# Per-head sums of six row groups moved from TensorE matmuls to SBUF-to-SBUF copies and VectorE adds

## The chip, the core and the metric

One core of one Trainium2 chip runs the whole program. The metric is the device time of one execution in microseconds (us).

## The reference, cut to what matters

Two layers, each an attention block A and a dense block B, over 2048 rows of 1024 values. Every row attends, in 32 heads of 32 channels, to eight rows: itself and the rows 2, 4, ..., 14 above.

```python
x = x + _A_ref(_layernorm(x), A_wqkv, A_wo)      # and again for layer 2
x = x + _B_ref(_layernorm(x), B_w1, B_b1, B_w2, B_b2)
# A: q, k, v = split(x @ wqkv); W, dil = 8, 2
logits = einsum("bhsd,bhswd->bhsw", q, kg) * Dh ** -0.5    # kg: k of the 8 rows
o = einsum("bhsw,bhswd->bhsd", softmax(logits), vg)        # then o @ wo
# B: gelu(x @ w1 + b1) @ w2 + b2, with F = 3584
```

## The kernel before

The rows are cut into groups of 512; `n` = 0 to 7 counts them, four in each layer. Tiles in PSUM take the results of TensorE; the other tiles here lie in SBUF. A group goes through four stages on TensorE: `gen_qkv`, `gen_wo`, `gen_ffn1`, `gen_ffn2`. Stages of different groups alternate, so that TensorE has matmuls while VectorE does the attention of another group. From group 1 on the order is wo(n), qkv(n+2), FFN1(n), FFN2(n). A stage yields after every unit of matmuls (8 matmuls in qkv, wo and FFN1; 7 in FFN2), and `sides` lists what is emitted after which unit. `hold()` makes all later VectorE instructions follow the last one emitted; otherwise the scheduler may reorder, and then each engine runs its list in order.

The channels lie so that the four partitions 4h to 4h+3 hold head h, in eight chunks `c`. A logit is therefore a sum over chunks, made by VectorE in `new_prod`, and a sum over four neighbouring partitions: the head sum. Before, TensorE makes it with a 0/1 matrix `smat` of 128x32, one quarter of the array for each 128 rows of the group:

```python
def head_sum(n, last=True):
    ...                                       # L: a PSUM tile [128, 8, 128], f32
    prod = st[n]["prods"].pop(0)
    for wh in range(2):
        for tb in range(NTT):                 # NTT = 4
            mm(L[tb * H:(tb + 1) * H, wh * 4:(wh + 1) * 4, :], lhsT=smat[:],
               rhs=prod[:, wh * 4:(wh + 1) * 4, tb * P:(tb + 1) * P], start=start,
               stop=last, skip_group_check=True, tile_position=(0, tb * H))

def attend(n):                                # softmax over the 8 rows
    head_sum(n); L = s.pop("L")
    ...                                       # mask for the first rows
    mx = max over w of L;  e = L - mx         # VectorE
    act.activation(e[:], e[:], ACT.Exp, scale=SCALE)      # ScalarE
    z = sum over w of e;  a = e / z           # VectorE (cut)
# spread(n): a goes through DRAM to all channels, abc     (GpSimd's DMA queue)
# av(n, c):  oT[c] = sum over w of abc * v, 4 VectorE ops (the weighted sums)
```

The schedule that the change touches (`ln_a(n)` normalizes the rows of group n and transposes them by DMA into `xnT`, which qkv(n) needs):

```python
stage(gen_ffn1(0), sides=at(4, attend, 1) + at(4, spread, 1) + at(4, hold) + each(new_prod, 2, 2, 1, 0, 4) + each(av, 1, 6, 2))
stage(gen_ffn2(0), sides=at(0, ln_stats_ahead, 3) + at(15, hold) + each(new_prod, 2, 15, 1, 4, 8) + at(23, hold) + at(23, ln_a, 3, None, True))
for n in range(1, N - 2):
    stage(gen_wo(n), sides=at(0, spread, n + 1) if n > 1 else at(7, attend, 2))
    stage(gen_qkv(n + 2), sides=(at(0, spread, 2) if n == 1 else []) + each(av, n + 1, 0, 2, 0, 3))
    stage(gen_ffn1(n), sides=at(20 if n == 1 else 9, attend, n + 2) + each(av, n + 1, 8, 2, 3, 8))
    if n + 3 < N:
        stage(gen_ffn2(n), sides=at(2, ln_a, n + 3))
    ...
```

## Time and profile before

| | before |
|---|---|
| device time, median of 6 runs | 1237.99 us (1237.62 to 1238.59) |
| span of the profiled run | 1236.0 us |
| TensorE / VectorE / ScalarE / GpSimd busy | 99% / 68% / 25% / 7% |
| granted TensorE clock | 1.00 |

The engine totals on the profile's page: busy us, share of the span, instructions.

```profile
PE 1227.6 (99%) x5775; PEld 632.1 (51%) x5825; DVE 840.5 (68%) x868; ACT 303.8 (25%) x475; POOL 92.3 (7%) x214
```

TensorE (PE) is never short of work, so only work or waits taken from it can change the time. The waits of PE in the whole run (who waited for whom: us in total, times, longest):

```profile
PE L L118 <- DVE big L93: 1.1, 1, 1.1
PE acc L118 <- DVE big L93: 1.1, 1, 1.1
PE acc L118 <- ACT xnT L93: 0.6, 1, 0.6
```

The last two are at the very start. The first is the head sum of group 1, as PE's timeline shows (start us, length us, engine, line, operation, tiles, count, idle before):

```profile
159.41 0.62 PE L118 MATMUL L<-big,smat 128*32 128x512 bf16 x8 [1.06 <-DVE big L93]
159.96 5.35 PE L118 MATMUL acc<-xnT,wt 128*128 128x512 bf16 x24
```

What a head sum costs is best read where nothing else disturbs. In FFN1, ScalarE applies one GELU per 8 matmuls and always waits for PE. Its timeline around the head sum of group 4:

```profile
472.32 0.69 ACT L93 ACTIVATE hT<-acc,b1T 128x512 bf16<-128x512 f32 x1 [1.04 <-PE acc L118]
474.05 0.69 ACT L93 ACTIVATE hT<-acc,b1T 128x512 bf16<-128x512 f32 x1 [1.04 <-PE acc L118]
476.43 0.69 ACT L93 ACTIVATE hT<-acc,b1T 128x512 bf16<-128x512 f32 x1 [1.69 <-PE acc L118]
```

The starts are 1.727 us apart, but 2.38 us across the head sum: it costs TensorE 0.65 us, more than the 0.55 us between its first start (159.41) and the next matmul's (159.96) in the timeline above.

### The profile page before, as it was taken

What the parts mean: (1) busy time and instruction counts of PE and PEld (TensorE: products, weight loads), DVE (VectorE), ACT (ScalarE), POOL (GpSimd) and SP (SyncE); (2) the same over time, 40 slices, a digit from 0 to 9 for tenths busy, and PEclk for the clock granted to TensorE, in tenths of its full rate; (3) what the DMA queues carried; (4) which work ended last, traced back from release to release, by engine and by line L of the source; (5) the groups of instructions that cost most, each with busy time, mean ns of one, the idle gap of its engine ahead of it and who ended that gap; (6) DMA issues with size and microseconds to landing.
All of it is one profiled execution on the core that took longest, in us unless ns stands there. A gap on an engine that the chain in (4) does not pass through costs nothing.

```text
span 1236.0 us, 13961 instructions
## 1 busy us (share of the span) xinstructions
PE 1227.6 (99%) x5775; PEld 632.1 (51%) x5825; DVE 840.5 (68%) x868; ACT 303.8 (25%) x475; POOL 92.3 (7%) x214
## 2 busy tenths in 40 slices
PE   9999999999999999999999999999999999999998
PEld 6666544456444564445644455444654444444444
DVE  7999899987985899337994379853597787012001
ACT  3333152023420145101351023510234001300310
POOL 4010011002000100001000010000001002000000
PEclk9999999999999999999999999999999999999999
DMA  9954564576645555656556565666554567546441
GB/s 305 283 179 144 187 208 155 166 177 220 183 157 200 168 175 157 195 168 189 166 155 203 171 178 162 162 200 200 171 170 136 185 199 200 162 157 196 150 136 54
DMA packets 217440, 220.33 MB, mean 178 GB/s; under 512 B 68179, under 2 KB 187105, under 8 KB 214305
## 3 DMA queue, kind: packets, MB, share of 16 engines
q1 hardware_dynamic: 214704, 208.69, 54.4%
q0 software_dynamic: 2672, 10.76, 2.9%
q8 instruction: 45, 0.74, 0.2%
q14 instruction: 19, 0.15, 0.0%
HBM read 197.40 MB, written 6.29 MB: 165 GB/s over the span
## 4 chain that ended last, share of the span: by engine, by line
PE 96%; DVE 2%; DMA 1%; issue 0%; POOL 0%; ACT 0%; SPq 0%
PE acc L118 96%; DVE big L93 1%; DVE stats L93 1%; DMA x<-in_A_x_dram 1%; PE L L118 0%; POOL rstd L93 0%; DVE x L93 0%; DVE xn L93 0%; SPq L93 0%; DVE mv L93 0%; ACT xnT L93 0%; PE L L211 0%; ACT kT L93 0%; ACT vT L93 0%; POOL zhalo L93 0%
## 5 line engine op out<-in xcount | busy, mean ns | idle before, releaser
L118 PE MATMUL acc<-xnT,wt 128*128 128x512 bf16 (+1 forms) x3376 | 721.5, 376 | 0.6 <-ACT xnT L93 0.6
L118 PEld LDWEIGHTS <-wt 128*128 128x128 bf16 x3376 | 398.7, 119 | 321.0 <-issue 3.9
L118 PE MATMUL acc<-wt,hT 128*128 128x512 bf16 (+1 forms) x1780 | 386.0, 376 | 2.1
L118 PEld LDWEIGHTS <-hT 128*128 128x128 bf16 x1820 | 178.1, 98 | 209.0
L93 DVE TENSOR_TENSOR big<-big 128x1024 bf16<-128x1024 bf16 (+2 forms) x184 | 244.1, 1358 | 1.8
L93 ACT ACTIVATE hT<-acc,b1T 128x512 bf16<-128x512 f32 x224 | 151.5, 687 | 318.4 <-PE acc L118 317.8
L93 DVE TENSOR_TENSOR big<-abc,vT 128x4096 bf16<-128x4096 bf16 x64 | 143.9, 2282 | 48.2 <-DMA abc<-a_d 47.9
L93 DVE TENSOR_TENSOR tmp<-acc,b2bc 128x512 f32<-128x512 f32 x56 | 38.6, 690 | 179.1 <-PE acc L118 175.7
L93 DVE TENSOR_TENSOR big<-qT,kT 128x4096 bf16<-128x4096 bf16 x64 | 143.8, 2286 | 23.9 <-ACT kT L93 23.2
L93 ACT CAST qT<-acc 128x512 bf16<-128x512 f32 x64 | 37.2, 586 | 324.5 <-PE acc L118 324.5
L118 PE MATMUL acc<-wt,oT 128*128 128x512 bf16 x440 | 97.4, 379 | 0.4
L93 DVE BATCH_NORM_STATS2 stats<-x 128x6 f32<-128x512 bf16 x128 | 83.9, 678 | 4.4 <-DMA x<-in_A_x_dram 3.6
L118 PEld LDWEIGHTS <-oT 128*128 128x128 bf16 x448 | 43.8, 98 | 52.9
L93 DVE TENSOR_TENSOR x<-acc,big 128x512 bf16<-128x512 f32 (+1 forms) x9 | 5.7, 633 | 90.0 <-PE acc L118 90.0
L93 ACT CAST vT<-acc 128x512 bf16<-128x512 f32 x64 | 37.5, 586 | 84.1 <-PE acc L118 84.1
L93 ACT CAST kT<-acc 128x512 bf16<-128x512 f32 x64 | 37.5, 586 | 71.7 <-PE acc L118 71.7
L93 POOL TENSOR_TENSOR rstd<-mv,eps_t 128x1 f32<-128x1 f32 x60 | 14.5, 241 | 500.9 <-DVE mv L93 500.8
L93 POOL DMA_DIRECT2D a_d<-a x32 | 19.0, 620 | 416.3 <-DVE a L93 416.3
L93 DVE TENSOR_TENSOR x<-acc,x 128x512 bf16<-128x512 f32 x64 | 43.0, 671 | 7.8 <-PE acc L118 7.5
L93 DVE TENSOR_SCALAR xn<-x,mv,rstd 128x1024 bf16<-128x1024 bf16 x52 | 28.6, 550 | 27.3 <-POOL rstd L93 26.9
L93 DVE TENSOR_TENSOR x<-tmp,x 128x512 bf16<-128x512 f32 x56 | 38.6, 690 | 1.5
L93 POOL TENSOR_TENSOR rstd<-rstd,mhalf 128x1 f32<-128x1 f32 x60 | 33.8, 563 | 4.7
(54 smaller groups left out, 208.7 us busy)
## 6 DMA issues: line engine op xcount, KB each, us to landing
wt<-in_B_w_dram SPq DMA_DIRECT2D x56, 1024.0 KB, 5.6
wt<-in_B_w_dram SPq DMA_DIRECT2D x64, 896.0 KB, 4.7
wt<-in_A_wqkv_dram SPq DMA_DIRECT2D x46, 1024.0 KB, 5.4
wt<-in_A_wo_dram SPq DMA_DIRECT2D x16, 1024.0 KB, 5.0
abc<-a_d POOLq DMA_DIRECT2D x32, 256.0 KB, 4.4
x<-in_A_x_dram SPq DMA_DIRECT2D x16, 256.0 KB, 6.0
out_dram<-x SPq DMA_DIRECT2D x31, 128.0 KB, 1.7
wt<-in_A_wqkv_dram SPq DMA_DIRECT2D x4, 512.0 KB, 7.8
```

The source lines that it names most:

```text
L93: inst = f(*args, **kwargs)
L118: return pe(nc.tensor.matmul(*args, **kwargs))
```

## The change

The intent is to take the head sums of groups 2 to 7 from TensorE. The products get the layout [128, 4, 8, 128] (quarter of the group, window, row). For each quarter a copy from SBUF to SBUF puts the four partitions of a head side by side in one partition. Three VectorE adds finish the sum in SBUF. The softmax of groups 3 to 6 moves to FFN2, and there Exp gets a fixed place in ScalarE's order (`act.on`), as do two small copies in qkv that are not shown; a `hold()` goes before group 2's softmax in wo(1). Group 1's head sum stays on TensorE, one unit later. The second half of its weighted sums goes behind the first adds of FFN2(0) (the evictions of the first four accumulators). Thus group 2's products are complete before FFN2(0) and can be copied then.

```diff
+    def gather(n):
+        prod = s["prods"].pop(0)
+        Lq = bigp.tile([P, HP, W, P], BF16, name="big")
+        s["Lq"] = Lq
+        for tb in range(NTT):
+            pool.dma_start(Lq[tb * H:(tb + 1) * H, :, :, :], prod[:, tb, :, :])
 def attend(n):
+        if "Lq" in s:
+            vec.tensor_tensor(out=e[:], in0=Lq[:, 0, :, :], in1=Lq[:, 1, :, :], op=ALU.add)
+            for j in range(2, HP):
+                vec.tensor_tensor(out=e[:], in0=e[:], in1=Lq[:, j, :, :], op=ALU.add)
+            L = e
...
+        act.on = 1 < n < N - 1
         act.activation(e[:], e[:], ACT.Exp, scale=SCALE)
+        act.on = False
...
-    stage(gen_ffn1(0), sides=at(4, attend, 1) + at(4, spread, 1) + at(4, hold) + each(new_prod, 2, 2, 1, 0, 4) + each(av, 1, 6, 2))
-    stage(gen_ffn2(0), sides=at(0, ln_stats_ahead, 3) + at(15, hold) + each(new_prod, 2, 15, 1, 4, 8) + at(23, hold) + at(23, ln_a, 3, None, True))
+    stage(gen_ffn1(0), sides=at(5, attend, 1) + at(5, spread, 1) + at(5, hold) + each(new_prod, 2, 2, 1)
+          + at(10, gather, 2) + at(10, hold) + each(av, 1, 10, 2, 0, 4))
+    stage(gen_ffn2(0), sides=at(0, ln_stats_ahead, 3) + at(15, hold) + at(15, ln_a, 3, None, True) + each(av, 1, 16, 1, 4, 8) + at(23, hold))
...
-        stage(gen_ffn1(n), sides=at(20 if n == 1 else 9, attend, n + 2) + each(av, n + 1, 8, 2, 3, 8))
+        gather(n + 2)
+        stage(gen_ffn1(n), sides=(at(20, attend, n + 2) if n + 3 == N else []) + each(av, n + 1, 8, 2, 3, 8))
         if n + 3 < N:
-            stage(gen_ffn2(n), sides=at(2, ln_a, n + 3))
+            stage(gen_ffn2(n), sides=at(0, attend, n + 2) + at(2, ln_a, n + 3))
```

## The prediction

> **What bounds the kernel.** TensorE. The engine totals give PE 1227.6 us of 1236.0 (99%), VectorE 840.5 (68%), ScalarE 25%, at full granted clock in every slice; the chain of waits is 96% PE. PE's waits hold, after the start-up, one stall of note: 1.06 us where the head-sum matmuls of group 1 wait for VectorE's product tree (at 159.4 us). So only work or stalls taken from TensorE count.
>
> **What the change removes.** The head sums of groups 2 to 7: 8 matmuls each, 128x32 stationary, 4 column tiles. The chain shows 0.55 us for the eight. The full cost is in the cadence of ScalarE's GELUs in FFN1: one per 1.727 us, but 2.38 us across a head sum (342, 476, 629, 781, 934 us alike), so 0.65 us. Two passes of 0.214 us make 0.43; the other 0.2 us fits the Trainium skill, "TensorEngine Tiling (Array Packing)", Key Properties: changing the tiling mode drains the engine. Six head sums: 6 x 0.65 = 3.9 us, all on the critical path.
> Group 1's head sum stays on TensorE, but one unit of FFN1(0) later (1.73 us), which should hide its 1.06 us wait: the last product of group 1 ends at 159.4 us, and the new place is reached at about 160.0 us.
>
> **What it adds.** VectorE: three adds of 128x1024 per group. Float32 results of that size take 1.21 us today (a<-e,z), so 3.6 us a group, 22 us in all. The Trainium skill, "VectorE: DVE Perf Modes", tier table, gives float32 tensor_tensor no faster mode; the 1.21 us agrees. The products with the four-dimensional pattern should still take 2.29 us. DMA: 4 copies of 256 KB a group, about 0.6 us issue each on GpSimd, 4 to 6 us to land (estimate from abc<-a_d, 4.4 us), 6 MB beside 220. All off the critical path: in groups 4 to 6 VectorE idles over 40 us of each 152.
> The Exp of groups 3 to 6 moves from between GELUs to FFN2, where ScalarE is idle; GELU never stalled PE, so this is worth nothing.
>
> **Where it can be lost.** From 143 to 246 us VectorE is full. Before, group 1's weighted sums end at 222 us and products of group 2 fill 228 to 246. After, half the weighted sums end there: by my ledger at 246 to 248 us (same work, plus up to 2 us of normalization of group 3), while wo(1) begins at about 247 and needs the last of them 1.5 us later. I expect 0 to 2 us of PE stall, 0.5 on average. Second: attend(7) comes about 6 us later, so group 7's weighted sums press on the evictions of FFN2(5) and wo(6) near 1005 us; 4.5 us of VectorE idle there absorb most of it.
>
> **Predicted.** 1238.0 - 3.9 - 1.06 + 0.5 = 1233.6 us, 80% between 1231.8 and 1237.0. Chances: faster by over 2% 0.01, within 2% 0.97, slower by over 2% 0.02.
>
> **What would show it.** Right: 16 head-sum matmuls left; an even 1.727 us GELU cadence through FFN1(1) to FFN1(5); no PE wait at 160 us; VectorE busy up by about 20 us, PE busy down by 3 to 4; the period of groups 3 to 6 shorter by 0.65 us from 152.6. Wrong: PE waiting for oT at wo(1), or for accumulators at FFN2(1) or wo(6); adds longer than 1.3 us; products longer than 2.3 us.
>
> **What would make it wrong.** A schedule in which VectorE delays evictions, GpSimd's queue held by the gathers so that a normalization comes late, or a stall that now hides behind the head sums.

## The result, and the profile after

| | before | after |
|---|---|---|
| device time, median of 6 runs | 1237.99 us | 1232.85 us (1232.55 to 1233.35) |
| span of the profiled run | 1236.0 us | 1231.0 us |
| VectorE busy | 840.5 us | 869.1 us |

The ratio is 0.9959, with a 95% interval of 0.9946 to 0.9972. A ratio is the mean time of one kernel's fast runs over that of the other's of the same rounds, so it is not quite the ratio of the medians quoted. The gain of 5.1 us is clear of noise and within 2%.

Engine totals, PE's waits, PE around group 1's head sum, and the GELUs at the place shown of before:

```profile
PE 1226.2 (100%) x5777; PEld 631.8 (51%) x5777; DVE 869.1 (71%) x886; ACT 304.1 (25%) x475; POOL 126.4 (10%) x238
```

```profile
PE acc L118 <- DVE big L93: 1.1, 1, 1.1
PE acc L118 <- ACT xnT L93: 0.6, 1, 0.6
```

```profile
159.93 0.62 PE L118 MATMUL L<-big,smat 128*32 128x512 bf16 x8
160.48 4.71 PE L118 MATMUL acc<-xnT,wt 128*128 128x512 bf16 x21
```

```profile
473.22 0.69 ACT L93 ACTIVATE hT<-acc,b1T 128x512 bf16<-128x512 f32 x1 [1.04 <-PE acc L118]
474.95 0.69 ACT L93 ACTIVATE hT<-acc,b1T 128x512 bf16<-128x512 f32 x1 [1.04 <-PE acc L118]
476.67 0.69 ACT L93 ACTIVATE hT<-acc,b1T 128x512 bf16<-128x512 f32 x1 [1.04 <-PE acc L118]
```

The wait of group 1's head sum is gone, the cadence in FFN1 is even, and PE waits for nothing after the start. PE busy falls by only 1.4 us because about 50 matmul records are missing from the trace of before (5775 matmuls against 5825 weight loads); the comparison of positions is safer. After the change 16 head-sum matmuls are left, those of groups 0 and 1. FFN2(0) starts at 199.68 us before and 198.48 after (1.20 us earlier). The first eviction of qkv(5) and that of qkv(7), first in the kernel before, then in the changed one:

```profile
569.66 0.59 ACT L93 CAST qT<-acc 128x512 bf16<-128x512 f32 x1 [63.20 <-PE acc L118]
874.86 0.59 ACT L93 CAST qT<-acc 128x512 bf16<-128x512 f32 x1 [63.20 <-PE acc L118]
```

```profile
566.46 0.59 ACT L93 CAST qT<-acc 128x512 bf16<-128x512 f32 x1 [60.83 <-PE acc L118]
870.35 0.59 ACT L93 CAST qT<-acc 128x512 bf16<-128x512 f32 x1 [60.83 <-PE acc L118]
```

So the lead grows from 1.20 to 3.20 us over three head sums (2, 3, 4) and to 4.51 over five: 0.66 us each. Over the whole run it is 1.2 + 6 x 0.65 = 5.1 us, against 5.0 in the spans.

The new costs on VectorE. Groups by shape: busy us, mean ns of one, idle before.

```profile
L93 DVE TENSOR_TENSOR e<-e,big 128x1024 f32<-128x1024 f32 x12 | 14.4, 1201 | 0.1
L93 DVE TENSOR_REDUCE mx<-e 128x128 f32<-128x1024 f32 x6 | 11.5, 1910 | 0.1
L93 DVE TENSOR_TENSOR e<-big 128x1024 f32<-128x1024 bf16 x6 | 7.3, 1216 | 0.0
L93 DVE TENSOR_REDUCE mx<-L 128x128 f32<-128x1024 f32 x2 | 2.4, 1222 | 0.0
```

The three adds cost 3.6 us a group as predicted. The maximum, however, takes 1.91 us when its input is in SBUF and 1.22 us from PSUM, so VectorE's bill is 4.3 us a group.

### The profile page after: what moved, and what is told of

The parts are those of the page before. It is cut to its first block, busy times and chain, and to the rows that moved or that the text cites. A ratio compares the mean times of both kernels' runs of the same rounds, so it can differ in the third digit from the quotient of the medians.

```text
span 1231.0 us, 13956 instructions
## 1 busy us (share of the span) xinstructions
PE 1226.2 (100%) x5777; PEld 631.8 (51%) x5777; DVE 869.1 (71%) x886; ACT 304.1 (25%) x475; POOL 126.4 (10%) x238
## 4 chain that ended last, share of the span: by engine, by line
PE 99%; DVE 0%; DMA 0%; ACT 0%; POOL 0%; issue 0%
PE acc L118 99%; DMA x<-in_A_x_dram 0%; DVE stats L93 0%; PE L L118 0%; PE acc L211 0%; PE L L211 0%; ACT xnT L93 0%; DVE mv L93 0%; DVE x L93 0%; POOL rstd L93 0%
## 5 line engine op out<-in xcount | busy, mean ns | idle before, releaser
L93 DVE TENSOR_TENSOR big<-big 128x2048 bf16<-128x2048 bf16 (+2 forms) x184 | 245.5, 1359 | 2.9
L93 POOL TENSOR_TENSOR rstd<-mv,eps_t 128x1 f32<-128x1 f32 x60 | 23.5, 391 | 434.2 <-DVE mv L93 434.2
L93 POOL TENSOR_TENSOR rstd<-rstd,mhalf 128x1 f32<-128x1 f32 x60 | 43.8, 730 | 4.7
L93 POOL DMA_DIRECT2D big<-big x24 | 13.5, 568 | 256.0 <-DVE big L93 239.1
```

What stands on the lines that cost most here:

```text
L93: inst = f(*args, **kwargs)
```

## The experiments

**Theory**: the gain is TensorE time, six head sums of 0.65 us and one wait, and all that was added runs in VectorE's slack. **Rival**: the gain comes from where the softmax and the weighted sums now stand. All runs are compared with the kernel before on the same chip (its medians 1237.65 to 1237.78 us there), and with the changed kernel, which repeated at 1232.91 us (1232.56 to 1233.50). Only e11 ran on one chip with it; for the others that comparison goes across chips, on which the kernel before agreed within 0.13 us.

### e1_shift and e2_pe_sum: the two parts of the gain

e1 is the kernel before with one edit, e2 the changed kernel with one.

```diff
# e1_shift
-    stage(gen_ffn1(0), sides=at(4, attend, 1) + at(4, spread, 1) + at(4, hold) ...
+    stage(gen_ffn1(0), sides=at(5, attend, 1) + at(5, spread, 1) + at(5, hold) ...
# e2_pe_sum
     def gather(n):
+        return          # attend() then takes its head_sum() branch, on TensorE
```

> The kernel before, with only group 1's softmax (and its head sum on TensorE) one unit of FFN1(0) later. Theory (the gain is TensorE time: six head sums of 0.65 us and one wait): the 1.06 us wait at 159.4 us is gone, so 1.1 to 1.2 us faster than before, about 1236.8 us. Rival (the gain comes from moving the softmax and the weighted sums, which unloads VectorE and ScalarE): no change, 1238.0 us.

> The changed kernel, but the head sums of groups 2 to 7 stay on TensorE, at the new places, with no copies and no adds. Theory: six head sums at 0.65 us come back, 3.9 us slower than the changed kernel, about 1236.8 us. Rival: the new places make the gain, so it stays within 1 us of the changed kernel, 1232 to 1234 us.

Measured: e1 1236.60 us (1.2 us faster than before), e2 1236.73 us (3.8 us slower than the changed kernel). The 95% intervals of their ratios to before (0.9978 to 1.0002 and 0.9980 to 1.0003) just include 1, but none of their ten executions (1236.37 to 1237.14) reaches the eleven of before (1237.56 to 1238.69). The two parts add up: 1.2 + 3.8 = 5.0 of the 5.1 us. In e2's trace PE waits for nothing after the start, so the 3.8 us are matmul time and no new wait. The rival falls. e2 has every new place of the softmax and the weighted sums, and keeps no more of the gain than the one-unit shift alone gives.

### e5_twice: what is in the 0.65 us

```diff
# the kernel before, head_sum
-        for wh in range(2):
-            for tb in range(NTT):
+        for wh, tb in [(i // NTT, i % NTT) for i in range(2 * NTT)] * (2 if n > 1 else 1):
```

> The kernel before, with the eight head-sum matmuls of groups 2 to 7 issued twice in a row (the second time over the first, so the result is the same). It measures what the eight cost without entering and leaving the four-tile mode. Theory (0.65 us = 0.43 for two full passes and about 0.22 for the two changes of mode): the second eight cost 0.43 each, 6 x 0.43 = 2.6 us slower than before. Rival (each set of eight costs 0.65 by itself): 3.9 us slower.

Measured 1240.46 us, 2.8 us over before; the theory said 2.6 and the rival 3.9. GELUs around the doubled head sum of group 3:

```profile
341.09 0.69 ACT L93 ACTIVATE hT<-acc,b1T 128x512 bf16<-128x512 f32 x1 [1.04 <-PE acc L118]
343.90 0.69 ACT L93 ACTIVATE hT<-acc,b1T 128x512 bf16<-128x512 f32 x1 [2.12 <-PE acc L118]
```

The gap is 2.81 us, 1.08 above the normal 1.727. The second eight matmuls add 1.08 - 0.65 = 0.43 us, which is two full passes of 0.214 us: four tiles really run at once (one after another the eight would take 1.7 us). The other 0.22 us is paid once per visit, so a third of what each head sum costs is not its passes. That fits the Trainium skill, "TensorEngine Tiling (Array Packing)", Key Properties, which says that changing the tiling mode drains the engine. The drain itself is the page's reading. What the trace of before adds is that weight loads, which elsewhere follow one another after 0.1 us on average, pause for 0.42 us on both sides of the head sum:

```profile
340.33 0.12 PEld L118 LDWEIGHTS <-smat 128*32 128x32 bf16 x8 [0.42 <-issue]
340.88 0.33 PEld L118 LDWEIGHTS <-wt 128*128 128x128 bf16 x3 [0.42 <-issue]
```

Whether the change of mode or only the held-up weight loads cost the 0.22 us, no run tells apart.

### e7_late: how near the predicted stall was

The prediction charged 0.5 us for group 1's weighted sums arriving late at wo(1). None was seen: the last of them ended at 247.74 us.

```diff
# the changed kernel, av(n, c)
-        vec.tensor_tensor(out=pv[:], in0=s["abc"][:] ...
+        for _ in range(2 if (n, c) == (1, 7) else 1):
+            vec.tensor_tensor(out=pv[:], in0=s["abc"][:] ...
```

> The changed kernel, with the first product of group 1's last weighted sum done twice (2.2 us more of VectorE just ahead of wo(1)). In the changed kernel that sum ends at 247.74 us and its weights are loaded for wo(1) at about 248.1 us, so the slack should be 0.4 us. Theory: TensorE waits 1.8 us there, 1.8 us slower than the changed kernel, about 1234.7 us. Rival (more slack than the trace shows): no change.

Measured 1234.54 us, 1.6 us slower than the changed kernel. PE waits for `oT` at exactly that place:

```profile
249.47 0.39 PE L118 MATMUL acc<-wt,oT 128*128 128x512 bf16 x1 [0.78 <-DVE oT L93]
250.53 12.47 PE L118 MATMUL acc<-wt,oT 128*128 128x512 bf16 x57 [0.67 <-DVE oT L93]
```

The 2.2 us added became 1.6 us of time, so the slack was about 0.6 us. The term of the prediction was a real hazard that missed by about half a microsecond.

### e3_ffn1: the softmax back in FFN1

```diff
# the changed kernel
-        act.on = 1 < n < N - 1
+        act.on = False
-        stage(gen_ffn1(n), sides=(at(20, attend, n + 2) if n + 3 == N else []) + ...
+        stage(gen_ffn1(n), sides=at(20 if n == 1 else 16, attend, n + 2) + ...
-            stage(gen_ffn2(n), sides=at(0, attend, n + 2) + at(2, ln_a, n + 3))
+            stage(gen_ffn2(n), sides=at(2, ln_a, n + 3))
```

> The changed kernel, but the softmax of groups 3 to 6 is placed in FFN1 again and its Exp runs between GELUs, without the fixed order on ScalarE. Theory: GELU has slack, so the time stays at 1232.9 us within 0.3 us. Rival (moving Exp and its two table loads of 1.28 us out of FFN1 is worth time): slower by 0.5 us or more, up to 4 x 2.5 us.

Measured 1234.26 us, 1.4 us slower: the expectation failed. ScalarE and PE in FFN1(2):

```profile
487.56 1.28 ACT L93 ACT_TABLE_LOAD   x1
495.70 1.06 ACT L93 ACTIVATE e<-e 128x1024 f32<-128x1024 f32 x1 [6.87 <-DVE e L93]
496.78 1.28 ACT L93 ACT_TABLE_LOAD   x1
498.07 4.15 ACT L93 ACTIVATE hT<-acc,b1T 128x512 bf16<-128x512 f32 x7
...
498.81 5.34 PE L118 MATMUL acc<-xnT,wt 128*128 128x512 bf16 x24 [1.64 <-ACT hT L93]
```

Exp stood in ScalarE's list ahead of GELUs that were ready, and waited 6.87 us there for VectorE. With the two table loads around it no GELU ran from 487.5 to 498.1 us. The six accumulators filled up and PE stopped for 1.64 us, its only wait after the start. In the kernel before, Exp stood between the same two table loads, its longest wait for VectorE was 1.8 us, and PE did not stop. So what is new is the wait of 6.87 us, not the table loads, though they lengthen the stop: with the longer chain on VectorE, Exp must not stand between GELUs. In the changed kernel it runs at 504.57 us, after the last GELU. The run changes both the place and the fixed order; which of the two suffices is not told apart.

### e4, e8, e9: half of the weighted sums behind the first adds

e4 is the changed kernel with the order of before in FFN1(0) and FFN2(0): all of av(1) first, then products 4 to 7 of group 2, its gather, and the normalization of group 3. e8 puts that normalization early again. e9 keeps it late and delays the gather.

```diff
# e4_av_ahead
-          + at(10, gather, 2) + at(10, hold) + each(av, 1, 10, 2, 0, 4))
+          + each(av, 1, 6, 2))                       # with each(new_prod, 2, 2, 1, 0, 4)
-    ... at(15, hold) + at(15, ln_a, 3, None, True) + each(av, 1, 16, 1, 4, 8) + at(23, hold))
+    ... at(15, hold) + each(new_prod, 2, 15, 1, 4, 8) + at(23, gather, 2) + at(23, hold) + at(23, ln_a, 3, None, True))
# e8_ln_early, against e4
+    ... at(15, hold) + at(15, ln_a, 3, None, True) + each(new_prod, 2, 15, 1, 4, 8) + at(23, gather, 2) + at(23, hold))
# e9_gather_late, against e4
-    ... + at(23, gather, 2) ...
+    wo(1): at(6, gather, 2)      qkv(3): at(4, hold) + at(4, attend, 2) + at(4, spread, 2), av(2) from unit 5
```

> The changed kernel, but with the order of before in FFN1(0) and FFN2(0): all of group 1's weighted sums ahead of the first adds of FFN2(0), the second half of group 2's products behind them, its copies after those. Theory: group 2's rows come some 45 us later, but are only needed at 265 us, so the time stays at 1232.9 us within 0.4 us. Rival (the split of the weighted sums is needed): VectorE waits for the copies in front of work that TensorE needs at wo(1) or FFN1(1), 1 us slower or more.

> As e4_av_ahead, but the normalization of group 3 stands right behind the first adds of FFN2(0), as in the changed kernel, so that its transposing copies land before the head-sum copies of group 2 are issued at about 248 us. Theory (in e4 the transposing copies and the head-sum copies ran into each other, 15 us instead of 4 to 5, and VectorE waited for them in front of the evictions of FFN2(0)): the 10.6 us wait of TensorE is gone, 1232.9 us within 0.4 us. Rival (the late products themselves are what costs): still 5 us or more slower than the changed kernel.

> As e4_av_ahead (normalization of group 3 late, as in the kernel before), but the head-sum copies of group 2 are issued at the seventh unit of wo(1), about 12 us later, and its softmax five units into the next stage. Theory (in e4 the head-sum copies slow the transposing copies of group 3, and nothing else is at fault): TensorE's 10.6 us wait is gone although the normalization stays late; 1233 to 1234 us. Rival (the late normalization is at fault by itself): still 5 us or more slower than the changed kernel.

e4 measured 1243.01 us (1239.4 to 1247.3), some 10 us slower than the changed kernel: a clear miss. The six executions fall into 1239.4 to 1240.2 and 1245.8 to 1247.3; the trace is of one at 1245.81. VectorE, then PE, near wo(1):

```profile
265.69 0.55 DVE L93 TENSOR_SCALAR xn<-x,mv_ahead,rstd_ahead 128x1024 bf16<-128x1024 bf16 x1 [13.18 <-DMA xnT<-xn]
266.15 0.68 DVE L93 TENSOR_TENSOR x<-tmp,x 128x512 bf16<-128x512 f32 x1
...
268.08 5.88 PE L118 MATMUL acc<-wt,oT 128*128 128x512 bf16 x16 [10.59 <-DVE tmp L93]
```

The fourth normalization needs the first of the three `xn` buffers back and waits 13.18 us for its transposing copy. Behind it, in VectorE's order, stand the evictions that TensorE needs. The DMA issues of e4 from 230 to 262 us, with the median time to landing last:

```profile
big<-big POOLq DMA_DIRECT2D x4, 256.0 KB, 15.2
xnT<-xn SPq DMA_TRANSPOSE x3, 17.6
```

Before, the same three transposing copies at the same place landed in 6.9 us (issues of before, 245 to 256 us):

```profile
xnT<-xn SPq DMA_TRANSPOSE x3, 6.9
```

e8 and e9 part the two sets of copies in opposite ways, and in both PE's wait of 10.6 us at wo(1) is gone. In e8 the head-sum copies land in 7.5 us and PE waits 0.53 us; the time is 1233.40 us, half a microsecond over the changed kernel and just beyond the 0.4 expected; the executions of the two overlap. In e9 the late normalization waits 2.09 us as it did before. That settles it for this place: the wait came from the head-sum copies meeting the transposing copies. Why they slow each other so much the runs do not show.

e9 as a whole was 1247.80 us, not the 1233 to 1234 expected. Another wait opened at FFN2(1), some 130 us later:

```profile
386.67 23.50 PE L118 MATMUL acc<-wt,hT 128*128 128x512 bf16 x98 [8.88 <-DVE tmp L93]
```

Group 2's softmax ended 14 us later than in the changed kernel (296 us against 283), its weighted sums as well, and these, with the adds of group 3's softmax behind them, stand ahead of FFN2(1)'s evictions on VectorE. In e8 group 2's products are as late as in e4, but its copies are issued at 251 us and its softmax starts when it does in the changed kernel (265.5 us against 265.8), and the loss is only half a microsecond. So the copies must come neither at the same time as the transposes nor as late as in e9. The early products themselves, for which half of the weighted sums was moved, are worth about half a microsecond; of e4's 10 us nearly all comes from the place of group 3's normalization, which brings its transposes together with the copies.

A long wait also costs more than itself. Windows of e4 right after its wait (us, length, busy time and count of PE, PEld, DVE, ACT, POOL, granted clock, DMA share, GB/s):

```profile
268.10:270.00 1.90, 1.90 (x5) 0.67 (x5) 1.90 (x5) 0.00 (x0) 0.75 (x2) 0.50 0.21 47
270.00:272.00 2.00, 2.00 (x6) 0.71 (x5) 2.00 (x4) 0.00 (x0) 0.00 (x0) 0.50 0.00 0
272.00:274.00 2.00, 2.00 (x9) 0.84 (x8) 2.00 (x5) 0.00 (x0) 0.85 (x2) 0.82 0.00 0
```

After the wait the granted clock is 0.50 for about 4 to 5 us. The Trainium skill, "TensorE: Matmul & The Clock Gate", Part 1, says that after an idle window of about 3.4 us the array falls to half rate and needs about as long under load to return. The trace agrees as far as it goes: after 10.6 us without work the clock is 0.50, and the return takes 4 to 5 us, somewhat longer than the page's figure. Where the threshold lies these runs do not show; waits of 7.65 us (e10) and 8.88 us (e9) also left the clock at 0.50. Half rate for 4 to 5 us costs some 2 to 2.5 us (an estimate), and the span of e4 is 13.1 us over the changed kernel's, with 10.6 us of waiting. The waits of 1.5 to 1.8 us in the next experiment leave the clock at 1.00.

### e6_adds2: how much slack VectorE has

```diff
# the changed kernel, attend(n)
+            for _ in range(2):
                 ...   # the three adds
```

> The changed kernel, with the three adds of each of groups 2 to 7 done twice: 3.5 us more of VectorE per group, 21 us in all. Theory (VectorE has slack where the adds now stand): 1232.9 us within 0.3 us, at most 1 us more if the evictions of FFN2(1) come late. Rival (VectorE is close to the limit, the adds eat part of the gain): a good part of 3.5 us per group, 5 us slower or more.

Measured 1239.47 us (1236.7 to 1240.1), 6.6 us slower where at most 1.3 was expected. All waits of PE after the start in this run:

```profile
379.80 1.67 PE L118 MATMUL acc<-wt,hT 128*128 128x512 bf16 x7 [1.48 <-DVE tmp L93]
383.27 19.80 PE L118 MATMUL acc<-wt,hT 128*128 128x512 bf16 x91 [1.80 <-DVE tmp L93]
961.08 1.89 PE L118 MATMUL acc<-xnT,wt 128*128 128x512 bf16 x8 [0.30 <-ACT hT L93]
992.15 19.80 PE L118 MATMUL acc<-wt,hT 128*128 128x512 bf16 x91 [0.48 <-DVE tmp L93]
1041.61 48.51 PE L118 MATMUL acc<-xnT,wt 128*128 128x512 bf16 x224 [1.73 <-DVE x L93]
```

Groups 4 to 6 absorb 3.5 us more without a wait (no wait between 384 and 961 us). Groups 2 and 3 cannot, at FFN2(1), nor can group 7, around FFN2(5) and the last wo stages. The waits add up to 5.8 us of a span that is 7.2 us longer; the rest is not attributed. "Off the critical path" thus holds for the adds as they are; at the two ends their room is less than as much again.

### e10_group1, e11_group1b, e12_after: one more head sum

Group 1's head sum is done by copies and adds as well; two products of group 2 go behind its weighted sums, into wo(1), with the gather behind them, and group 3's softmax goes behind the first adds of FFN2(1).

```diff
# e10_group1, against the changed kernel
+    gather(1)
-    FFN1(0): at(5, attend, 1) + ... + each(new_prod, 2, 2, 1) + at(10, gather, 2) + ...
+    FFN1(0): at(2, new_prod, 2, 0) + at(3, ln_stats_ahead, 3) + at(5, attend, 1) + ... + each(new_prod, 2, 6, 1, 1, 6) + ...
+    wo(1): each(new_prod, 2, 5, 1, 6, 8) + at(7, hold) + at(7, gather, 2)    qkv(3): at(8, attend, 2) + ...
+    FFN2(1): at(17, attend, 3)
# e11_group1b, against e10
+    FFN2(0): ... each(av, 1, 16, 1, 4, 8) + at(23, hold) + at(23, ln_a, 3, None, True)
+    FFN2(1): at(15, hold) + each(av, 2, 15, 1, 6, 8) + at(17, attend, 3)
```

> An attempt at a better version: group 1's head sum by copies and adds too, two of group 2's products put behind group 1's weighted sums to make room on VectorE, group 3's softmax behind the first adds of FFN2(1). Theory: one more head sum off TensorE, 0.65 us faster than the changed kernel (1232.2 us) if VectorE keeps group 1's weighted sums ahead of wo(1), where the slack was 0.4 us; with a wait there it is the size of the wait slower. Rival (what limits now is VectorE around wo(1)): slower than 1233 us.

> A second attempt at a better version: e10_group1 with its two waits addressed. The normalization of group 3 goes behind group 1's weighted sums again (2 us less in front of wo(1), where TensorE waited 1.4 us for them), and the last two weighted sums of group 2 and the softmax of group 3 go behind the first adds of FFN2(1) (where TensorE waited 7.7 us for those adds). Theory (only these two places were short of VectorE time): both waits gone or under 0.3 us, one more head sum off TensorE than in the changed kernel, 1232.2 us. Rival (VectorE has no room left for 4.4 us more before wo(2), so the wait moves elsewhere): 1233.5 us or more.

> The changed kernel unaltered, beside the run above, to compare on one chip: 1232.9 us within 0.3 us, 0.41% faster than before, no wait of TensorE after the start.

e10 measured 1243.47 us: PE waits 7.65 us for evictions at FFN2(1) and about 1.4 us at wo(1). e11 measured 1234.06 us, e12 1232.91 us. In the trace of e11 (its slowest execution, 1234.93 us) the wait at FFN2(1) is gone, but one of 1.65 us opens at wo(1):

```profile
249.67 0.70 DVE L93 TENSOR_TENSOR tmp<-acc,b2bc 128x512 f32<-128x512 f32 x1
250.27 2.29 DVE L93 TENSOR_TENSOR big<-qT,kT 128x4096 bf16<-128x4096 bf16 x1
252.47 0.55 DVE L93 TENSOR_SCALAR xn<-x,mv_ahead,rstd_ahead 128x1024 bf16<-128x1024 bf16 x1
252.92 0.70 DVE L93 TENSOR_TENSOR x<-tmp,x 128x512 bf16<-128x512 f32 x1
253.52 0.70 DVE L93 TENSOR_TENSOR x<-acc,x 128x512 bf16<-128x512 f32 x1
...
254.27 8.79 PE L118 MATMUL acc<-wt,oT 128*128 128x512 bf16 x40 [1.65 <-DVE x L93]
```

A product of 2.29 us was scheduled between two halves of an eviction. Without that wait this execution would have taken 1233.3 us (an estimate, 1234.93 - 1.65); its trace also has four waits of 0.2 to 0.3 us, three of which the repeat of the changed kernel does not have, so what the seventh head sum would bring cannot be read from it. So neither attempt beats the changed kernel, and whether a seventh head sum pays stays open.

## Why the prediction was right

The prediction said 1233.6 us (1231.8 to 1237.0); measured were 1232.85.

- **TensorE is the bound, and only its work counts**: right. After the change PE waits for nothing after the start.
- **Six head sums of 0.65 us**: right. Positions give 0.66 us each, e2 3.8 us for the six, and e5 splits one into 0.43 and 0.22 us as predicted.
- **The wait of 1.06 us hidden by one unit**: right, 1.2 us in e1 and in the positions. Where the other 0.14 us come from stays open.
- **0.5 us of stall at wo(1)**: the mis-sized term. It was 0; e7 shows a slack of about 0.6 us. This is most of the 0.75 us between forecast and result. The end of the weighted sums, "at 246 to 248 us", was right at 247.74. The second risk, group 7's weighted sums near 1005 us, did not show either: PE waits nowhere there.
- **Adds of 1.21 us, products unchanged at 2.29 us**: right (1.20 to 1.22 and 2.286 us). The tier table of the Trainium skill, "VectorE: DVE Perf Modes", gives float32 `tensor_tensor` no faster mode, which agrees. Missed was the maximum, which takes 0.7 us longer from SBUF. The profile of before held the hint, since the sum over `e`, also from SBUF, took 1.92 us there against 1.22 us for the maximum from PSUM. VectorE's busy time rose by 28.6 us, not 20.
- **Copies landing in 4 to 6 us**: too low, 7.8 us (median). It cost nothing where they stand; in e4, where they met the transposing copies, both slowed and 10 us were lost.
- **"All off the critical path"**: true of the changed kernel, but the margin was overrated. e6 shows that it is below 3.5 us at FFN2(1) and at the end.
- **"Moving Exp is worth nothing"**: right of the kernel before: e2 has the Exp of groups 3 to 6 in FFN2 and is no faster than e1, which has it between GELUs. It is wrong of the changed kernel: e3 shows 1.4 us for the place and the fixed order together, since the longer softmax would have Exp hold up GELUs.

## What to carry to other kernels

Where one engine is busy all the time, the gain of moving work off it can be read from the cadence of an undisturbed consumer; here the 0.65 us between GELUs gave the result to a few tenths. Such a gain is only kept if everything that the moved work lengthens is moved out of the way too: instructions that wait in order ahead of ready ones (Exp among GELUs), copies that meet other copies, evictions behind long vector work. A piece that looks worthless in a diff may be what keeps a gain of 5 us from becoming a loss of 5: here it is the normalization of group 3, called 8 units earlier (e4 against e8).

## What the Trainium skill lacked or had wrong

- "TensorEngine Tiling (Array Packing)", Key Properties, says that a change of tiling mode drains the engine, but not what that costs. Here 0.22 us a visit are left for going to four column tiles and back, if nothing else is in them.
- "VectorE: DVE Perf Modes", tier table, gives `tensor_reduce` the same 1x from SBUF and PSUM. Over 1024 float32 elements read with a stride of 128 elements it takes 1.91 us from SBUF and 1.22 us from PSUM. The skill speaks of strided reads from SBUF elsewhere, but gives no time for them on VectorE.
- "DMA: Bandwidth & Descriptors", Rules for kernel authors, says that a DMA transpose next to ordinary DMAs needs nothing. That is about correctness, and all results here are correct; but in e4 transposing copies took 17.6 us instead of the 6.9 us of before beside 1 MB of copies within SBUF, and those 15.2 us instead of the 7.5 us of e8.
